# From the fourth step of a chunked scan on, each step's output products and the next step's Gram products form one set on the tensor engine

## The chip, the core and the metric

The kernel runs on one core of a Trainium2 chip. Its time is the device time of one execution in microseconds (us), here the median of three runs. The engines of the core work side by side and wait for one another through semaphores: PE (TensorE, matrix products; PEld is its weight loads), DVE (VectorE), ACT (ScalarE), POOL (GpSimd) and SP (SyncE, which issues the transfers). PSUM is the memory into which PE writes.

## The reference, cut to what matters

```python
# scan: 4 batches x 8 heads, 768 positions, head size 32, state size 16, in chunks
cum = np.cumsum(la, axis=-1)                       # la = log a of the chunk
L = np.exp(cum[:, :, :, None] - cum[:, :, None, :]) * causal
M = np.einsum('bhin,bhjn->bhij', Cc, Bc) * L       # the Gram products, then the decays
y[:, :, sl] = einsum(M, xc) + einsum(Cc, state) * exp(cum)
state = decay_full * state + sum_j(Bc * xc * decay_from_j)
# then, on the 3072 x 256 rows of y:
xn = x / rms * rms_g
x = (silu(xn @ w_gate) * (xn @ w_val)) @ w_out     # layer 1, d_ff 1536
h = x @ w_in
out = (s * relu(h)**2 + b) @ w_out2                # layer 2, d_ff 2048
```

## The kernel before

**The scan** goes in 16 steps of 48 positions. A step has two units (`NPAIR`; unit c belongs to step c // 2), each of which holds two batches with all 8 heads. A step consists of four functions, which `stream` lists in this order:

- `scan`: DVE's scan instruction makes the decays of the step in `a_sb`.
- `gram`: PE multiplies B by C (tiles `raw_bc`; `first_bc` in steps 0 and 1) into the columns 0 to 255 of both PSUM banks of the unit's tile `y`; then DVE multiplies these by the decays into `m`, four instructions for the two units (two 384 wide, two 128 wide).
- `outs`: PE multiplies `m` by the x tile `xh`, which also holds the state in 16 of its rows, into columns 256 to 511 of the first bank of `y`. ACT copies the new state into the next step's `xh` (`keep_state`), and DVE, POOL and ACT scale the rows to `xn`.
- `turn`: PE transposes `xn` against `ident` into columns 256 to 511 of the second bank, and ACT and DVE take these out as `xth` and `xtl`, the high and the low part of layer 1's input.

**The layers.** Layer 1 goes over the tokens in 7 blocks (4, 4, 4, 5, 5, 5, 5 units), each in 12 parts (products into `h`, then into `o`). Block 0 runs in plain float32 with weights `w1f`, which DVE and ACT decode from 64-bit words while it runs; the later blocks run as three products of split numbers (`w1h`, `w1l`). Layer 2 follows with tiles `h` and `acc`. The scan's steps lie between the products of the blocks whose tokens do not depend on them; the last `turn` of a block has to be done before that block's first product.

**The order of the instructions** is not that of the program text. Every call is recorded by a `Plan`, with a price and with the calls that it depends on; for PSUM it counts dependences by whole banks. `Plan.issue` then runs a list schedule over engines and transfers and issues the calls of each engine in the order of that schedule. Where it sees PE idle in the first microseconds, it puts in small bfloat16 products without a use (line 354). All other instructions have the line of the one call that issues them (358). `bundled` gives the small products of a step one group name, so that the planner keeps them together: "g" for Gram products, "o" for output products, "t" for transposes. The first product of a group takes over the dependences of all its members, with 0.6 us to spare.

The products of a group use the array in small pieces, which the trace prints as rows*columns: 32*64 for Gram products (16*64 in steps 0 and 1), 64*64 for output products, 128*128 for everything of the layers and for the transposes.

The Gram products read `raw_bc`, one buffer for all steps (398): a step's twelve transfers into it can start only when the Gram products of the step before have read it. The tile `y` comes from a pool of two buffers. Each unit asks for a new tile in `gram`, and so waits for everything that the unit two before it did with its tile.

Of the kernel before, what the change touches and what calls it, by code (L numbers as in the profile page):

```python
# [8 lines left out]
F32 = mybir.dt.float32  # L9
# [10 lines left out]
P = 128  # L20
# [8 lines left out]
NPAIR = 2  # L29
NUNIT = CPB * NPAIR  # L30
# [7 lines left out]
BLOCK = [j for j, n in enumerate(BLOCKS) for _ in range(n)]  # L38
NB = [n * UT for n in BLOCKS]
LAG = 2  # L40
F1 = 12
F2 = 16
N2 = 512
# [317 lines left out]
def place(k, h):  # L361

    return h % 2 * 4 + h // 2 if k % CPB < FREE // NPAIR else h


def chunk(c, z):

    p = c % NPAIR
    return (2 * p + (z ^ p)) * CPB + c // NPAIR
# [3 lines left out]
def scan_glu_relu2(ctx: ExitStack, tc: tile.TileContext, bc, xr, aa, cst, w1, w2, gn, sv, bv, out):  # L373
# [3 lines left out]
    const = ctx.enter_context(tc.tile_pool(name="const", bufs=1))  # L377
    wts = ctx.enter_context(tc.tile_pool(name="wts", bufs=F1))
    wlo = ctx.enter_context(tc.tile_pool(name="wlo", bufs=F2))
# [9 lines left out]
    s_p = ctx.enter_context(tc.tile_pool(name="s", bufs=3))  # L389
    hl_p = ctx.enter_context(tc.tile_pool(name="hl", bufs=LAG + 1))  # L390
    res_p = ctx.enter_context(tc.tile_pool(name="res", bufs=1))
    ps_h = ctx.enter_context(tc.tile_pool(name="ps_h", bufs=2, space=PS))
    ps_o = ctx.enter_context(tc.tile_pool(name="ps_o", bufs=1, space=PS))
    ps_y = ctx.enter_context(tc.tile_pool(name="ps_y", bufs=2, space=PS))
# [15 lines left out]

    w1h = [wts.tile([P, 6, P], F32R, tag="w1h", name="w1h") for m in range(F1)]
    w1f, w1l, w2f, w2h = {}, {}, {}, {}
# [6 lines left out]
    a_t, x_t, m_t, y_t, xn_t = {}, {}, {}, {}, {}  # L419
# [26 lines left out]
    def group(p, par):  # L446
        at = (2 * p + par) * 32
        return slice(at, at + NST)
# [23 lines left out]
    def load_x(c):  # L472
        t = x_p.tile([P, DM], F32, tag="xh", name="xh")
        for z in range(2):
            queue = nc.scalar if c < NPAIR else nc.sync
            queue.dma_start(out=t[z * R + NST:(z + 1) * R], in_=xr[chunk(c, z)])
            if c < NPAIR:
                nc.gpsimd.memset(t[z * R:z * R + NST], 0.0)
        x_t[c] = t
# [16 lines left out]
    def bundled(name, units, products, together=False):  # L496
        if units[0] >= FREE:
            nc.bundle = f"{name}{units[0]}"
        nc.fresh = True
        if together:  # L500
            products(units)
        else:
            for c in units:
                products(c)
                nc.fresh = nc.fresh or units[0] < FREE
        nc.bundle = None

    def gram_of(c):
        return y_t[c][:, :, 0:4 * R].rearrange("p a (b r) -> p a b r", b=4)

    def gram_products(units):
        g = [gram_of(c) for c in units]
        if units[0] < FREE:
            for q in range(NH // 2):
                for z in range(2):
                    for p in range(NPAIR):
                        for par in range(2):
                            rows = group(p, par)
                            nc.tensor.matmul(
                                out=g[p][z * R:(z + 1) * R, par, q],  # L520
                                lhsT=first_bc[rows, z ^ p, q * R:(q + 1) * R],
                                rhs=first_bc[rows, z ^ p, (4 + q) * R:(5 + q) * R], start=True, stop=True,
                                tile_position=((2 * p + par) * 32, z * R),
                            )
            return
        for q in range(2):
            cols = slice(q * R, (q + 1) * R)
            for z in range(2):
                for p in range(NPAIR):
                    for half in range(2):  # L530
                        at = (2 * p + half) * 32
                        raw = raw_bc[at:at + 32, z ^ p]
                        nc.tensor.matmul(
                            out=g[p][z * R:(z + 1) * R, half, 2 * q:2 * q + 2], lhsT=raw[:, 0, cols],
                            rhs=raw[:, 1:3, cols], start=True, stop=True, tile_position=(at, z * R),
                        )

    def gram(units):
        if units[0]:
            load_bc(units)  # L540
        for c in units:
            y_t[c] = ps_y.tile([P, 2, 512], F32, tag="y", name="y")
        bundled("g", units, gram_products, True)
        for c in units:
            g = gram_of(c)
            t = a_t.pop(c)
            m = att2.tile([P, NH, R], F32, tag="m", name="m")
            mv, tv = (v.rearrange("p (a b) r -> p a b r", a=2) for v in (m, t))
            nc.vector.tensor_tensor(out=mv[:, :, :, NST:R], in0=g[:, :, :, NST:R], in1=tv[:, :, :, 0:CH], op=ALU.mult)
            nc.vector.tensor_tensor(  # L550
                out=mv[:, :, :, 0:NST], in0=g[:, :, :, 0:NST],
                in1=tv[:, :, :, CH:AW].to_broadcast([P, 2, 4, NST]), op=ALU.mult,
            )
            m_t[c] = m

    def rows_of(c):
        return y_t[c][:, 0, 4 * R:4 * R + DM]

    def out_products(units):
        for h in range(NH):  # L560
            for c in units:
                for z in range(2):
                    rows, t = slice(z * R, (z + 1) * R), z ^ c % NPAIR
                    nc.tensor.matmul(
                        out=rows_of(c)[t * R:(t + 1) * R, h * HD:(h + 1) * HD],
                        lhsT=m_t[c][rows, place(chunk(c, 0), h)], rhs=x_t[c][rows, h * HD:(h + 1) * HD],
                        start=True, stop=True,
                    )

    def keep_state(c):  # L570
        for z in range(2):
            t = z ^ c % NPAIR
            copy = nc.scalar.copy if c >= NPAIR else nc.vector.tensor_copy
            copy(out=x_t[c + NPAIR][z * R:z * R + NST], in_=rows_of(c)[t * R:t * R + NST])

    def outs(units):
        for c in units:
            if c < NPAIR:
                load_x(c)
        for c in units:  # L580
            if c + NPAIR < NUNIT:
                load_x(c + NPAIR)
        if units[0] < FREE:
            nc.fresh = True
            for c in units:
                out_products([c])
                nc.fresh = True
        else:
            bundled("o", units, out_products, True)
        ss = att2.tile([P, NPAIR], F32, tag="ss", name="ss")  # L590
        if units[0] == 0:
            nc.first_back = len(nc.ops) - 1
        for c in units:
            if c + NPAIR < NUNIT:
                keep_state(c)
            xn = xn_t[c] = att2.tile([P, DM], F32, tag="xn", name="xn")
            nc.scalar.activation(
                out=xn, in_=rows_of(c), func=AF.Square, scale=DM ** -0.5, accum_out=ss[:, c % NPAIR:c % NPAIR + 1]
            )
        if units[0] == 0:  # L600
            nc.squares = len(nc.ops) - 1
        rs = att2.tile([P, NPAIR], F32, tag="rs", name="rs")
        nc.now_free = units[0] < FREE
        nc.vector.tensor_scalar(out=ss, in0=ss, scalar1=1e-6, scalar2=None, op0=ALU.add)
        nc.gpsimd.tensor_tensor(out=rs, in0=ss, in1=mhalf.to_broadcast([P, NPAIR]), op=ALU.pow)
        if units[0] == 0:

            nc.vector.tensor_copy(out=held, in_=rs)
            nc.held = len(nc.ops) - 1
        for c in units:  # L610
            nc.scalar.activation(out=xn_t[c], in_=rows_of(c), func=AF.Copy, scale=rs[:, c % NPAIR:c % NPAIR + 1])
# [134 lines left out]
    def out1(j, m, hi, lo):  # L746
# [3 lines left out]
        for t in range(2):  # L750
            three(o[t], w1h[m][:, 4 + t, :], w1l[m][:, 4 + t, :], hi, lo, m == 0, m == F1 - 1)
            if m == F1 - 1:
                evac1(o, t, j)
# [29 lines left out]
    def hidden1_plain(j, m, half):  # L783
# [13 lines left out]
        def out():  # L797
            o = [t[:, :NB[j]] for t in o_t[j, 1]]
            last = m == F1 - 1
            for t in range(2):  # L800
# [158 lines left out]
    def drain(n):  # L959
        while len(pending) > n:  # L960
            pending.popleft()()
# [64 lines left out]
    behind = 3  # L1026
    for i in range(F1 + behind):
        if i < F1:
            decode1(i)
            hidden1_plain(0, i, 0)  # L1030
            drain(LAG)
        tokens_to(count[1] + (count[3] - count[1]) * (i + 1) // behind if i < behind else
                  count[3] + (count[7] - count[3]) * (i + 1 - behind) // F1)
        if i >= behind:
            hidden1_plain(0, i - behind, 1)
            drain(LAG)

# [6 lines left out]
    for i, (layer, j, m) in enumerate(plan):  # L1044
# [13 lines left out]
        if layer == 2:  # L1058
            if m == 0 and (g := j + 1) * N2 < 2 * NPAIR * SEQ:
                split_rows(g)  # L1060
            if m % 2 == 0:
                seven(j, m // 2)
                drain(LAG)
            continue
        hidden1(j, m)
        drain(LAG)
        for (i0, n0), (i1, n1) in zip(marks, marks[1:]):
# [76 lines left out]
```

## Time and profile before

| | |
|---|---|
| median of 3 runs (range) | 633.78 us (631.43 to 634.2) |
| the profiled execution: its own time | 633.83 us |
| the profiled execution: span from first to last instruction | 631.8 us |
| PE busy | 621.4 us, 98% of the span |
| DVE busy | 484.2 us, 77% |
| ACT busy | 446.2 us, 71% |
| sets of Gram products in 32*64 pieces | 14 (steps 2 to 15) |

The profiled execution's own time is 2.0 us longer than its span, and close to the median. A product's row in the trace lasts longer than the array needs for it, since products overlap in the pipeline: what a product costs is read from the start of one row to the start of the next.

### The profile page before, as it was taken

Reading aid. Unit: us, or ns where it says so; the run is one execution under the profiler, and the core shown is the slowest. Engines: PE = TensorE matmul, PEld = TensorE weight load, DVE = VectorE, ACT = ScalarE, POOL = GpSimd, SP = SyncE. Lnnn points to the kernel's source line nnn. Section 1 sums busy time; section 2 is a strip of 40 time slices with the busy share of each in tenths; the row PEclk is TensorE's granted clock in tenths of the full one; section 3 lists DMA queues with packets and bytes.
Section 4 is the critical chain, followed back from the end, with each engine's and each line's share of the span. In section 5 each row is a group of like instructions: output and inputs, shape, how many; then the busy total and the mean of one; then the engine's idle time right before and its main releaser. Section 6 shows DMA issues by size and latency. Waiting matters only on the chain.

```text
span 631.8 us, 12985 instructions
## 1 busy us (share of the span) xinstructions
PE 621.4 (98%) x4979; PEld 556.4 (88%) x4979; DVE 484.2 (77%) x980; ACT 446.2 (71%) x940; POOL 50.6 (8%) x88
## 2 busy tenths in 40 slices
PE   8999999999999999999999999999999999999996
PEld 7899999999988888888888889999999999999986
DVE  7999956677757666756775568798897897987975
ACT  3797535666646545655655479899898898988985
POOL 3000000000101111101232220000000000000000
PEclk9899999999999999999999999999999999999999
DMA  7769203343413432500100000001010010010101
GB/s 224 211 221 269 62 1 61 85 96 91 114 35 89 90 91 59 138 15 4 40 2 1 0 2 1 1 1 35 1 34 1 2 34 1 4 32 1 34 1 34
DMA packets 33694, 35.00 MB, mean 55 GB/s; under 512 B 14048, under 2 KB 30048, under 8 KB 33632
## 3 DMA queue, kind: packets, MB, share of 16 engines
q1 hardware_dynamic: 32688, 33.71, 20.6%
q8 instruction: 39, 0.64, 0.4%
q10 hardware_dynamic: 944, 0.46, 0.2%
q14 instruction: 23, 0.19, 0.1%
HBM read 30.90 MB, written 3.25 MB: 54 GB/s over the span
## 4 chain that ended last, share of the span: by engine, by line
PE 95%; DVE 2%; ACT 1%; issue 0%; DVEq 0%
PE h L358 54%; PE o L358 22%; PE acc L358 13%; PE y L358 5%; PE o L354 1%; DVE w1f L358 1%; DVE e L358 0%; ACT xn L358 0%; PE ab L358 0%; DVE res L358 0%; DVE a_sb L358 0%; DVE xh L358 0%; ACT e L358 0%; ACT xth L358 0%; ACT xh L358 0%
## 5 line engine op out<-in xcount | busy, mean ns | idle before, releaser
L358 ACT CAST hi<-s 128x256 fp32r<-128x256 f32 (+2 forms) x168 | 79.1, 474 | 69.8 <-DVE s L358 67.6
L358 ACT ACTIVATE s<-h 128x512 f32<-128x512 f32 (+2 forms) x168 | 96.1, 572 | 35.4 <-PE h L358 32.3
L358 PE MATMUL h<-x1h,w2h 128*128 128x512 f32 x384 | 119.2, 392 | 0.0
L358 DVE TENSOR_TENSOR lo<-s,hi 128x256 fp32r<-128x256 f32 (+2 forms) x168 | 85.7, 511 | 30.0 <-ACT hi L358 27.2
L358 PE MATMUL h<-xtl,w1h 128*128 128x480 f32 (+1 forms) x288 | 106.7, 371 | 0.0
L358 PE MATMUL h<-xth,w1l 128*128 128x480 f32 (+1 forms) x288 | 106.6, 370 | 0.0
L358 PE MATMUL h<-xth,w1h 128*128 128x480 f32 (+1 forms) x288 | 106.1, 369 | 0.1
L358 PE MATMUL acc<-hi,w2c 128*128 128x256 f32 x448 | 82.0, 281 | 0.0
L358 PEld LDWEIGHTS h<-x1h,w2h 128*128 128x128 f32 x384 | 69.2, 188 | 12.2
L358 DVE TENSOR_TENSOR s<-h,s 128x480 f32<-128x480 f32 (+1 forms) x72 | 44.6, 619 | 43.7 <-PE h L358 43.5
L358 PE MATMUL h<-x1l,w2h 128*128 128x512 f32 x192 | 75.0, 391 | 0.0
L358 PEld LDWEIGHTS acc<-hi,w2c 128*128 128x128 f32 x448 | 71.0, 189 | 2.2
L358 DVE TENSOR_TENSOR added<-s 128x256 f32<-128x256 f32 x144 | 56.4, 419 | 13.5 <-ACT s L358 12.5
L358 PE MATMUL acc<-lo,w2c 128*128 128x256 f32 x224 | 63.2, 282 | 0.0
L358 ACT ACTIVATE s<-s 128x512 f32<-128x512 f32 x96 | 60.2, 633 | 1.9
L358 PEld LDWEIGHTS h<-xth,w1h 128*128 128x128 f32 x288 | 54.1, 188 | 6.6 <-DVE s L358 0.5
L358 PEld LDWEIGHTS h<-xtl,w1h 128*128 128x128 f32 x288 | 54.1, 188 | 6.3 <-issue 1.0
L358 PEld LDWEIGHTS h<-xth,w1l 128*128 128x128 f32 x288 | 54.1, 188 | 6.4 <-issue 0.5
L358 PE MATMUL o<-lo,w1h 128*128 128x480 f32 (+1 forms) x144 | 53.0, 368 | 0.0
L358 PE MATMUL o<-hi,w1l 128*128 128x480 f32 (+1 forms) x144 | 52.9, 368 | 0.0
L358 PE MATMUL o<-hi,w1h 128*128 128x480 f32 (+1 forms) x144 | 52.9, 367 | 0.0
L358 DVE TENSOR_TENSOR lo<-added,hi 128x768 fp32r<-128x768 f32 x48 | 45.9, 956 | 0.6 <-ACT hi L358 0.5
(98 smaller groups left out, 1093.2 us busy)
## 6 DMA issues: line engine op xcount, KB each, us to landing
raw<-in_w SPq DMA_DIRECT2D x12, 768.0 KB, 4.9
raw<-in_w SPq DMA_DIRECT2D x16, 512.0 KB, 3.5
a_sb<-a_scr SPq DMA_DIRECT2D x28, 196.0 KB, 3.8
xh<-in_xr SPq DMA_DIRECT2D x60, 48.0 KB, 1.9
raw_bc<-in_bc SPq DMA_DIRECT2D x56, 32.0 KB, 2.2
raw_bc<-in_bc SPq DMA_DIRECT2D x112, 16.0 KB, 2.9
out_t<-res SPq DMA_DIRECT2D x13, 96.0 KB, 1.8
out_t<-res SPq DMA_DIRECT2D x5, 144.0 KB, 2.1
```

Source lines behind the costliest of these rows:

```text
L354: self.nc.tensor.matmul(out=idle, lhsT=ones, rhs=ones, start=True, stop=True)
L358: getattr(engine, op["fn"])(*op["args"], **op["kw"])
```

## The change

`JOIN` is the first unit of step 4. Up to step 3, nothing but the tile changes. For steps 4 to 15 the Gram products of a step are no longer issued in its own `gram`; they stand in the `outs` of the step before, ahead of that step's output products and in the same group. With them the loads of `raw_bc` are recorded there. The two tiles `y` are taken once and stay for all steps, so that only accesses to the same bank order the steps.

```diff
+JOIN = 4 * NPAIR
...
-    def gram(units):
+    y_p = [ps_y.tile([P, 2, 512], F32, tag="y", name="y") for _ in range(NPAIR)]
+
+    def begin_gram(units):
         if units[0]:
             load_bc(units)
         for c in units:
-            y_t[c] = ps_y.tile([P, 2, 512], F32, tag="y", name="y")
-        bundled("g", units, gram_products, True)
+            y_t[c] = y_p[c % NPAIR]
+
+    def gram(units):
+        if units[0] < JOIN:
+            begin_gram(units)
+            bundled("g", units, gram_products, True)
...
         else:
-            bundled("o", units, out_products, True)
+            ahead = range(units[0] + NPAIR, units[0] + 2 * NPAIR)
+            if JOIN <= ahead[0] < NUNIT:
+                begin_gram(ahead)
+
+                def products(units):
+                    gram_products(ahead)
+                    out_products(units)
+                bundled("o", units, products, True)
+            else:
+                bundled("o", units, out_products, True)
```

The planner then makes another order on every engine. Three places of it follow.

**Place 1, steps 10 and 11.** On PE before: the Gram products of step 10 (`y<-raw_bc`), eleven products of layer 1, and the output products of step 10 (`y<-xh,m`).

```order
L358 MATMUL y<-raw_bc 64x128 x16
L358 MATMUL h<-xtl,w1h 128x480
L358 MATMUL h<-xth,w1h 128x480 x2
L358 MATMUL h<-xth,w1l 128x480
L358 MATMUL h<-xtl,w1h 128x480
L358 MATMUL o_509<-hi,w1h 128x480
L358 MATMUL o_509<-hi,w1l 128x480
L358 MATMUL o_509<-lo,w1h 128x480
L358 MATMUL o_510<-hi,w1h 128x480
L358 MATMUL o_510<-hi,w1l 128x480
L358 MATMUL o_510<-lo,w1h 128x480
L358 MATMUL y<-xh,m 64x32 x32
```

On PE after the change, where step 10's output products stand: the Gram products of step 11 come directly ahead of them. (The planner counts a float32 product once, and the trace twice: x16 here is x32 there.)

```order
L359 MATMUL o_494<-lo,w1h 128x480
L359 MATMUL h<-xth,w1h 128x480
L359 MATMUL y<-raw_bc 64x128 x16
L359 MATMUL y<-xh,m 64x32 x32
L359 MATMUL h<-xth,w1l 128x480
L359 MATMUL h<-xtl,w1h 128x480
```

On DVE before, the four products `m` of step 10 stand well behind the four `xtl` of the turn before them:

```order
L358 SCALAR_TENSOR_TENSOR xtl<-y,sb,xth 128x2x48 x4
L358 TENSOR_SCALAR e<-raw_563 128x512
L358 TENSOR_TENSOR lo<-s,hi 128x480
L358 TENSOR_SCALAR raw_563<-raw_563 128x512
L358 SCALAR_TENSOR_TENSOR w2f<-raw_563 128x512
L358 TENSOR_TENSOR e<-e,sg 128x512
L358 TENSOR_TENSOR m<-y,a_sb 128x8x48 x2
L358 TENSOR_TENSOR m<-y,a_sb 128x8x16 x2
L358 TENSOR_TENSOR s<-h,s 128x480
```

On DVE after the change they stand around them:

```order
L359 TENSOR_TENSOR lo<-s,hi 128x480
L359 TENSOR_SCALAR raw_543<-raw_543 128x512
L359 TENSOR_TENSOR m<-y,a_sb 128x8x48 x2
L359 SCALAR_TENSOR_TENSOR xtl<-y,sb,xth 128x2x48 x4
L359 TENSOR_TENSOR m<-y,a_sb 128x8x16 x2
L359 TENSOR_TENSOR s<-h,s 128x480
```

So one set of products on PE has become a neighbour of another, and DVE's block at a turn has grown by the four `m`.

**Place 2, step 1, at 18 to 25 us of the trace.** On DVE before, from the second part's decode (`w1f`) to the first `m` of step 1:

```order
L358 TENSOR_SCALAR e<-raw_139 128x768
L358 TENSOR_TENSOR e<-e,sg 128x768
L358 SCALAR_TENSOR_TENSOR w1f<-raw_138 128x768
L358 TENSOR_TENSOR w1f<-w1f,e 128x768
L358 TENSOR_TENSOR h_157<-h,h_157 128x192
L358 TENSOR_TENSOR m<-y,a_sb 128x8x48
L358 TENSOR_SCALAR raw_139<-raw_139 128x768
L358 TENSOR_TENSOR e<-e,sg 128x768
```

On DVE after the change:

```order
L359 SCALAR_TENSOR_TENSOR w1f<-raw_140 128x768
L359 TENSOR_TENSOR e<-e,sg 128x768
L359 TENSOR_SCALAR e<-raw_141 128x768
L359 TENSOR_TENSOR h_157<-h,h_157 128x192
L359 TENSOR_TENSOR m<-y,a_sb 128x8x48
L359 TENSOR_SCALAR raw_141<-raw_141 128x768
L359 TENSOR_TENSOR w1f<-w1f,e 128x768
L359 TENSOR_TENSOR e<-e,sg 128x768
```

The instructions are the same; the second half of the decode, `w1f<-w1f,e`, has moved behind the first `m`. On PE the twelve products without a use that stood behind step 1's Gram products are gone.

**Place 3, the last turn of block 0's time (step 3), at 76 to 79 us.** On PE before, from the transposes to the first products of block 1 (`w1h`, `xth`):

```order
L358 MATMUL y<-ident,xn 128x128 x4
L358 MATMUL o_133<-h_269,w1f 128x192
L358 MATMUL o_134<-h_269,w1f 128x192
L358 MATMUL o_133<-h_277,w1f 128x192
L358 MATMUL o_134<-h_277,w1f 128x192
L358 MATMUL h<-xth,w1h 128x384
```

On PE after the change:

```order
L359 MATMUL o_135<-h_271,w1f 128x192
L359 MATMUL y<-ident,xn 128x128 x4
L359 MATMUL o_136<-h_271,w1f 128x192
L359 MATMUL o_135<-h_273,w1f 128x192
L359 MATMUL o_136<-h_273,w1f 128x192
L359 MATMUL h<-xth,w1h 128x384
```

One of the four output products that stood between the transposes and block 1 now stands ahead of the transposes.

## Rows read from the trace of the kernel before

**Rows 1.** What PE waited for, from 34 us to the end (total, times, longest); the largest.

```profile
PE h L358 <- ACT xth L358: 0.5, 1, 0.5
```

**Rows 2.** PE in order of time, step 10: start, us, instruction.

```profile
205.22 0.38 PE L358 MATMUL h<-xth,w1l 128*128 128x480 f32 x1
205.53 0.69 PE L358 MATMUL y<-raw_bc 32*64 32x128 f32 x32
206.15 0.49 PE L358 MATMUL h<-xtl,w1h 128*128 128x480 f32 x1
206.48 0.59 PE L358 MATMUL h<-xth,w1h 128*128 128x480 f32 x2
...
208.43 0.38 PE L358 MATMUL o<-lo,w1h 128*128 128x480 f32 x1
208.74 1.14 PE L358 MATMUL y<-xh,m 64*64 64x32 f32 x64
209.81 0.48 PE L358 MATMUL h<-xth,w1l 128*128 128x480 f32 x1
210.13 0.38 PE L358 MATMUL h<-xtl,w1h 128*128 128x480 f32 x1
```

**Rows 3.** PE: the last output product of steps 0 and 10, and what follows.

```profile
10.55 0.22 PE L358 MATMUL y<-xh,m 64*64 64x32 f32 x1
10.70 0.39 PE L358 MATMUL ab<-a_cl,ident 128*64 128x196 f32 x2
...
209.66 0.22 PE L358 MATMUL y<-xh,m 64*64 64x32 f32 x1
```

**Rows 4.** Front, step 1: PE, then DVE.

```profile
18.41 1.06 PE L358 MATMUL y<-first_bc 16*64 16x64 f32 x64
24.65 1.12 PE L358 MATMUL y<-xh,m 64*64 64x32 f32 x32 [1.30 <-DVE m L358]
27.55 2.29 PE L358 MATMUL h<-xth,w1f 128*128 128x192 f32 x6
29.63 1.15 PE L358 MATMUL o<-h,w1f 128*128 128x192 f32 x4
...
19.10 0.96 DVE L358 TENSOR_TENSOR w1f<-w1f,e 128x768 f32<-128x768 f32 x1
20.25 0.55 DVE L358 TENSOR_TENSOR m<-y,a_sb 128x384 f32<-128x384 f32 x1
```

**Rows 5.** Stretches: us, busy us of PE, PEld, DVE, ACT, POOL, granted clock, DMA share, GB/s.

```profile
26.90:30.30 3.40, 3.40 (x25) 3.34 (x22) 2.39 (x6) 1.67 (x6) 1.33 (x1) 0.50 0.83 139
50.00:60.00 10.00, 10.00 (x119) 9.73 (x119) 10.00 (x22) 7.74 (x18) 1.27 (x1) 1.00 0.95 273
```

**Rows 6.** PE from step 3's turn to block 1's first products.

```profile
76.87 1.47 PE L358 MATMUL o<-h,w1f 128*128 128x192 f32 x8
78.04 0.47 PE L358 MATMUL h<-xth,w1h 128*128 128x384 f32 x1
...
78.82 0.44 PE L358 MATMUL h<-xth,w1h 128*128 128x384 f32 x1
```

**Rows 7.** The page's transfers: KB each, median us from issue to landing.

```profile
raw_bc<-in_bc SPq DMA_DIRECT2D x112, 16.0 KB, 2.9
```

**Rows 8.** SP in order of time, step 10's loads: start, us until the last is issued.

```profile
194.84 5.14 SPq L358 DMA_DIRECT2D raw_bc<-in_bc  x9
```

**Rows 9.** The turn ahead of step 10 and step 10's `m`: PE, ACT, DVE.

```profile
201.95 0.60 PE L358 MATMUL y<-ident,xn 128*128 128x128 f32 x4
202.37 1.04 ACT L358 ACTIVATE xth<-y,sb 128x96 fp32r<-128x96 f32 x4 [0.96 <-PE y L358]
202.97 1.01 DVE L358 SCALAR_TENSOR_TENSOR xtl<-y,sb,xth 128x96 fp32r<-128x96 f32 x4
206.32 1.42 DVE L358 TENSOR_TENSOR m<-y,a_sb 128x384 f32<-128x384 f32 x4
```

## The prediction

> **What bounds the kernel now.** I read the table first: PE is busy for 98% of the span, DVE for 77%. That alone does not make PE the bound, so next come its waits. From 34 us to the end it waited twice; the longer wait was 0.5 us [rows 1]. So from there on the time is what PE's instruction stream costs, and only three things can change it: the cost of the stream itself, new waits, and the granted clock.
>
> The cost shows in the order of time around step 10. Only the starts of rows are used. Between 206.48 and 208.43 us nine products of 480 columns start (the order at place 1 lists them), so one costs 1.95 / 9 = 0.217 us [rows 2]. Around a set of small products the step from one start to the next is longer. The product ahead of the Gram set takes 0.31 (0.09 too much), the set 0.62, and the first product behind it 0.33 (0.11 too much): 0.82 us for one visit. The output set likewise: 0.31 (0.09), 1.07, 0.32 (0.10), together 1.26 us. A step pays 2.08 us for two visits, and 0.20 of this is the way out of the first and the way into the second.
>
> Ahead of 34 us it is otherwise. PE waits 1.30 us for DVE's `m` at 24.65 [rows 4], and from 26.90 to 30.30 it is busy throughout at a granted clock of 0.50, so 1.2 GHz in place of 2.4 [rows 5].
>
> **The merged sets.** Twelve Gram sets (steps 4 to 15) move next to the output products of the step before. One visit then costs 0.09 + 0.62 + 1.07 + 0.10 = 1.88 us, provided that the switch from Gram to output products costs what leaving a set costs. That switch is in no row, since the two sets never touch. The nearest rows are step 0's last output product, which steps to a product of another small shape (128*64) in 10.70 - 10.55 = 0.15 us, and step 10's, which steps to a full 128*128 product in 209.81 - 209.66 = 0.15 us [rows 3]. A change between two small shapes costs as much as one to the full array, and 32*64 to 64*64 is a change of shape too. So I let the switch stand inside the 0.62, and take 0.20 us for each merge: 12 x 0.20 = **-2.4 us**. The other bound: with no pause at the switch the step would be that inside the set, 1.07 / 64 = 0.017 us; 0.13 more each, 12 x 0.33 = -4.0 us.
>
> The Trainium skill ("TensorEngine Tiling (Array Packing)", Key Properties) says that a change of tiling mode, not merely of tile, drains the engine. By that the joined set keeps one drain in its middle and the gain is the smaller sum, -2.4 and not -4.0; the two 0.15 us steps agree.
>
> **The tiles and the transfers.** `y` had two buffers for two units before, so keeping them moves nothing in memory, and costs nothing as long as the same accesses are done in time. The twelve loads of `raw_bc` need the read of the last Gram set behind them. Nine of them took SP 5.14 us [rows 8], 0.57 each, so twelve take 6.9, and the last lands some 2.9 later [rows 7]: with about 0.9 us from the set's start to the first issue, 10.7 us. By the order after the change the closest two merged sets (with the output products of steps 12 and 13) stand 40 products of 480 columns apart: 40 x 0.217 + 1.88 + about 0.45 for the transposes = 11.0 us. It fits by 0.3 us. Two other pairs have 42 and 44 products, so 0.4 and 0.9 us more. Behind these loads on SP stand four `xh`, for a set a step later, and two `a_sb`. I take zero; a landing 1 us late at these places would cost 0.7 + 0.3 = 1.0 us.
>
> **The front.** At place 2 `w1f<-w1f,e`, 0.96 us at 19.10, moves behind the first `m`, which began at 20.25 [rows 4]. But `m` cannot start before the Gram set of 18.41 has ended at 19.47, so DVE may idle a little where it did not, and its last `m` there, for which PE waits at 24.65, comes later: I take **+0.25 us**, bounds 0 and +0.9 (the whole instruction's worth). The twelve products without a use that are gone filled time in which PE waited anyway. Whether the half-clock stretch behind stays is open: at half speed 3.4 us do the work of 1.7, so it is worth at most 1.7 us either way. The same long wait precedes it in both orders, so I leave it as it is. Further on DVE is full (10.00 of 10.00 us between 50 and 60 [rows 5]), and the Gram set of step 2 and others move by some products, but no DVE instruction is added, and PE did not wait there before; zero.
>
> **Block 1's start.** Between the last transposes of block 0 and block 1's first product stood eight rows of `o<-h,w1f` (place 3 lists them as four). They take 78.04 - 76.87 = 1.17 us, 0.146 each [rows 6]. After, six stand there. The first two products of block 1 took 78.82 - 78.04 = 0.78 us, where two of 384 columns cost 2 x 0.217 x 0.8 = 0.35, so PE already waited 0.43 us for `xth`. `xth` comes no sooner with two rows less ahead: that wait grows by 2 x 0.146, with the switch **+0.33 us**; bound 0, if ACT is done earlier.
>
> **The sum.** -2.4 + 0.25 + 0.33 = -1.8 us. The profiled execution's own time is 633.83, the median 633.78, so either gives **632.0 us**. 0.5% of this kernel is 3.2 us, about what a measurement can tell from no change: under 630.6 would be faster, over 636.9 slower. My forecast is no change that can be told.
>
> **Rivals.**
> *No pause at the switch.* Only the 0.15 us steps between other shapes speak against it. -4.0 + 0.58 gives 630.4.
> *The clock at the front.* If the 3.4 us at half clock do not come, 632.0 - 1.7 = 630.3. For it: DVE's order and PE's fill products both change just ahead. Against: PE still waits there. If a second such stretch comes, as fewer products run before it, 633.7.
> *The merged set is late (the other side).* A merged set must wait for the step's `m`, and its Gram products also until `xtl` has been read out of the second bank. Before, the four `m` (1.42 us) came well after the four `xtl` (1.01), with other work of DVE between; now they are one block of 2.43 us [rows 9]. ACT began on the turn 202.37 - 201.95 = 0.42 us after its start, DVE 1.02 after. So the block ends between 1.02 + 1.01 + 0.3 (the two small `m`) = 2.3 and 0.42 + 2.43 = 2.9 us after the transposes. By the order nine of the twelve merged sets stand only 12 to 21 products behind their transposes, that is 0.4 + 12 x 0.217 = 3.0 us at the least, and 3.6 at 15. One instruction of DVE that runs over (`lo`, `s`: 0.65 us) uses this up, and every product of the layers behind the set waits too. From 0.2 us of waiting per merge the gain is gone; 0.3 at nine sets costs 2.7 and gives 634.7; 0.6 gives 637.4, slower. For it: DVE's block is closer than any before. Against: DVE is free for a quarter of the span, and PE waited nowhere for `m` after 34 us. The loads above add up to 1.0 at three sets, which alone decides nothing.
> *It does nothing.* If the way in and out is paid all the same inside the joined set, only the front's +0.58 and other shifts remain: 634.
>
> **Chances.** The forecast 0.50 (own range 630.8 to 633.4); no pause 0.12; no half-clock stretch 0.10; a second one 0.08; late sets 0.15, of which 0.07 beyond 636.9; nothing 0.05. Faster: 0.12 + 0.10 and a little of the forecast's edge, 0.24. Slower: 0.07 and a little for waits that I do not see, 0.09. Same: 0.67. The range has to reach the no-pause and no-stretch cases below and the small late sets above: 629.8 to 635.4. It leaves out both lower cases at once and the large waits.
>
> **What would show it.** Twelve rows of `y<-raw_bc` directly followed by `y<-xh,m`, with 0.31 before, about 1.7 for both, 0.32 behind. Right on the switch if the last Gram product steps to the first output product in 0.15 to 0.2 us, wrong if in under 0.05. Right on the waits if PE waits in no more than 1 us in all behind 34 us, wrong if `y<-raw_bc` or `y<-xh,m` carry waits for `m`, `xtl` or a transfer. At the front: the wait for `m` some 0.25 longer, the clock 0.50 for about 3.4 us. At block 1: some 0.75 us in place of 0.43 ahead of its second product. A clock below 1.00 elsewhere, or waits at the merged sets of over 0.2 us each, would make the forecast wrong.

## The result, and the profile after

The changed kernel takes 636.46 us (median of 10 runs, 635.41 to 638.59), the kernel before 633.54 us beside it (10 runs, 631.23 to 634.68): a ratio of 1.0058, 95% interval 1.0044 to 1.0073. It is slower by 0.6%. I had forecast 632.0 us and a range up to 635.4. The profiled execution took 635.41 us with a span of 633.6; against the one of before (633.83 and 631.8) that is 1.6 us more by its own time and 1.8 by the span.

PE's waits from 34 us on, the counterpart of [rows 1] (what waited, for what, total, times, longest):

```profile
PE h L359 <- DVE s L359: 0.7, 1, 0.7
PE y L359 <- DVE xtl L359: 0.6, 1, 0.6
PE h L359 <- ACT xth L359: 0.5, 1, 0.5
PE h L359 <- ACT h L359: 0.2, 1, 0.2
PE h L359 <- DVE h L359: 0.2, 1, 0.2
```

They add up to 2.2 us, where before there were 0.7 (0.5 and 0.2), and the prediction asked for no more than 1. This list shows only gaps in which PE had nothing in flight; most of the loss stands in none of its lines, as will be seen.

**The joined set costs what was forecast.** PE in order of time, where step 10's output products follow step 11's Gram products (start, us, instruction), for [rows 2]:

```profile
208.57 0.38 PE L359 MATMUL h<-xth,w1h 128*128 128x480 f32 x1
208.88 0.69 PE L359 MATMUL y<-raw_bc 32*64 32x128 f32 x32
209.51 1.14 PE L359 MATMUL y<-xh,m 64*64 64x32 f32 x64
210.57 0.49 PE L359 MATMUL h<-xth,w1l 128*128 128x480 f32 x1
210.90 0.38 PE L359 MATMUL h<-xtl,w1h 128*128 128x480 f32 x1
```

The steps are 0.31 in, 0.63, 1.06, and 0.33 out, against 0.217 for a product: 0.09 + 0.63 + 1.06 + 0.11 = 1.89 us for 2.08 before. The Gram products' 0.63 is as long as when a full-size product followed (0.62): the way out of the small pieces is paid at the switch too. The last Gram product steps to the first output product in 0.20 us, as forecast:

```profile
209.31 0.27 PE L359 MATMUL y<-raw_bc 32*64 32x128 f32 x1
209.51 0.26 PE L359 MATMUL y<-xh,m 64*64 64x32 f32 x4
```

What the prediction cites from the Trainium skill ("TensorEngine Tiling (Array Packing)", Key Properties), that a change of tiling mode drains the engine, agrees with these 0.20 us.

**The turn.** ACT, then DVE, then PE around the turn at 107.5 us and the joined set behind it (for [rows 9]; the number in brackets is how long the engine idled ahead of the row, and for whom):

```profile
107.94 0.34 ACT L359 ACTIVATE xth<-y,sb 128x96 fp32r<-128x96 f32 x1 [0.55 <-PE y L359]
108.91 0.57 ACT L359 ACTIVATE xth<-y,sb 128x96 fp32r<-128x96 f32 x2 [0.62 <-DVE m L359]
110.11 0.34 ACT L359 ACTIVATE xth<-y,sb 128x96 fp32r<-128x96 f32 x1 [0.63 <-DVE m L359]
...
108.31 0.56 DVE L359 TENSOR_TENSOR m<-y,a_sb 128x384 f32<-128x384 f32 x1 [1.82 <-ACT xth L359]
109.51 0.56 DVE L359 TENSOR_TENSOR m<-y,a_sb 128x384 f32<-128x384 f32 x1 [0.64 <-ACT xth L359]
109.99 1.03 DVE L359 SCALAR_TENSOR_TENSOR xtl<-y,sb,xth 128x96 fp32r<-128x96 f32 x4
110.94 0.48 DVE L359 TENSOR_TENSOR m<-y,a_sb 128x128 f32<-128x128 f32 x2
...
107.52 0.60 PE L359 MATMUL y<-ident,xn 128*128 128x128 f32 x4
111.43 0.99 PE L359 MATMUL y<-raw_bc 32*64 32x128 f32 x32
```

Before, the four `xth` ran in one piece of 1.04 us [rows 9]. Now ACT and DVE take turns: `xth`, `m`, `xth` twice, `m`, `xth`, one behind the other, although neither `m` nor `xth` needs what the other makes. Both read the second bank of the same tile `y`. The waits are in the issued program: of the 64 `m` in the trace, 17 carry a wait for ACT's semaphore, before none; of the 64 `xth`, 23 carry one for DVE's, before 8. So the last `m` ends at 111.42, 3.9 us after the transposes began, and the joined set begins at 111.43 and is stretched to 0.99 - 0.69 = 0.30 us more than the one above. The waits of ACT for `m` in the whole scan, 34 to 330 us (total, times, longest):

```profile
ACT xth L359 <- DVE m L359: 7.1, 14, 0.6
```

And of DVE, for the same stretch:

```profile
DVE a_sb L359 <- DMA a_sb<-a_scr: 10.2, 9, 2.1
DVE m L359 <- ACT xth L359: 7.6, 14, 1.8
```

The two waits for one another are in neither list of before; the wait for the decays was there, with 6.8 us in 6.

When the last `m` of a step ends is what decides. In the changed kernel four of the twelve joined sets are stretched, by 0.26 to 0.41 us. They are the four (at 111.4, 159.0, 253.9 and 265.1 us) whose last `m` ends less than 0.2 us ahead of the set's first product, or after it. At the other eight it has ended 0.4 us before or earlier, and each of these costs 1.88 or 1.89 us.

**Two places where it ends on PE.** At 214 us DVE's scan waits for its load; the `xtl` and `s` behind it are late, and PE's next `h` waits (order of time on DVE, then PE):

```profile
214.11 0.97 DVE L359 TENSOR_TENSOR_SCAN a_sb<-a_sb,delta 128x392 f32<-128x392 f32 x1 [2.08 <-DMA a_sb<-a_scr]
219.88 0.65 DVE L359 TENSOR_TENSOR s<-h,s 128x480 f32<-128x480 f32 x1
...
220.58 0.49 PE L359 MATMUL h<-xth,w1h 128*128 128x480 f32 x1 [0.70 <-DVE s L359]
```

And the last step's output products, which now stand 11 products behind their turn (23 before), find `xtl` unfinished (PE in order of time):

```profile
315.71 1.57 PE L359 MATMUL y<-xh,m 64*64 64x32 f32 x64 [0.62 <-DVE xtl L359]
```

**The front and block 1.** For [rows 4], PE at step 1's first output products:

```profile
24.58 1.12 PE L359 MATMUL y<-xh,m 64*64 64x32 f32 x32 [1.71 <-DVE m L359]
```

For [rows 5], the stretch at half clock (us, busy of PE, PEld, DVE, ACT, POOL, granted clock, DMA share, GB/s):

```profile
26.90:30.30 3.40, 3.40 (x23) 3.34 (x22) 2.31 (x6) 1.65 (x5) 1.33 (x1) 0.52 1.01 296
```

For [rows 6], PE from block 0's last output products into block 1:

```profile
79.30 1.14 PE L359 MATMUL o<-h,w1f 128*128 128x192 f32 x6
80.14 0.47 PE L359 MATMUL h<-xth,w1h 128*128 128x384 f32 x1
80.45 0.33 PE L359 MATMUL h<-xth,w1l 128*128 128x384 f32 x1
80.61 0.34 PE L359 MATMUL h<-xth,w1h 128*128 128x384 f32 x1
```

Step 1's output products start 0.07 us earlier than before, not 0.25 later (PE's wait for `m` is 0.41 longer, 1.71 for 1.30, since PE comes to it earlier); the clock does the same; and block 1's first two products take 80.61 - 80.14 = 0.47 us for 0.78 before.

**Where PE's time went.** The layers' products are the same in both kernels and come in the same order, so they can be counted. For each row of PE I take the step to the next row's start, less what a product of its kind takes (0.163 us for 192 columns, 0.175 for 384, 0.2175 for 480), 0.82, 1.26 or 1.88 us for a Gram set, an output set or a joined set, and 0.44 or 0.22 for four or two transposes. What is left is lost time. Its growth over the kernel before, between numbered products (their times in the changed kernel's trace below them):

```
products              0-48   48-480  480-840  840-1260  1260-1500 | 48-1500  joined  time 48-1500
up to (us)            34     119     196      301       358
changed kernel        0.0    1.0     0.5      2.0       1.1       | 4.6      12      +2.2
```

The last column is the time by which product 1500 comes later, counted from product 48. It is 4.6 lost less 12 x 0.20 by the way the loss is worked out, so the sum itself proves nothing; that a joined set costs 1.88 is read from the sets' own rows. Behind product 1500 PE's rows run alike; what follows PE's last product is 0.3 us shorter, so the spans differ by 1.8 us.

### The profile page after: what moved, and what is told of

It reads as the page before. It is cut to its first block, busy times and chain, and to the rows that moved or that the text cites. A ratio compares the mean times of both kernels' runs of the same rounds, so it can differ in the third digit from the quotient of the medians.

```text
span 633.6 us, 12944 instructions
## 1 busy us (share of the span) xinstructions
PE 621.5 (98%) x4967; PEld 556.8 (88%) x4967; DVE 484.2 (76%) x980; ACT 447.5 (71%) x940; POOL 54.0 (9%) x88
## 4 chain that ended last, share of the span: by engine, by line
PE 85%; DVE 7%; ACT 3%; DMA 2%; issue 1%; POOL 0%; SPq 0%; DVEq 0%; POOLq 0%
PE h L359 48%; PE o L359 19%; PE acc L359 13%; PE y L359 4%; DMA a_sb<-a_scr 2%; DVE w1f L359 1%; DVE e L359 1%; DVE a_sb L359 1%; ACT xth L359 1%; DVE m L359 1%; PE o L355 1%; DVE xtl L359 1%; ACT xn L359 1%; DVE raw L359 1%; DVE s L359 0%
```

## The experiments

All medians are of 10 to 12 runs beside the kernel before on the same chip (6 for e7), ratios to it with 95% intervals.

| run | median | ratio (95%) |
|---|---|---|
| e1 tiles kept, no joins | 633.38 | 0.9984 (0.9970 to 0.9997) |
| e2 m after xth | 635.89 | 1.0037 (1.0025 to 1.0049) |
| e3, e5 early m | 633.34, 633.31 | 0.9988 (0.9972 to 1.0004), 0.9999 (0.9985 to 1.0013) |
| e4, e14 joins from step 9 | 636.06, 636.01 | 1.0029 (1.0013 to 1.0044), 1.0035 (1.0017 to 1.0053) |
| e13 the same, m after xth | 634.01 | 0.9998 (0.9980 to 1.0016) |
| e6, e15 the same, early m | 632.0, 632.84 | 0.9979 (0.9963 to 0.9995), 0.9987 (0.9971 to 1.0004) |
| e7 decays loaded first | 648.54 | 1.0233 (1.0205 to 1.0261) |
| e8 early m, two decay buffers | 631.58 | 0.9976 (0.9961 to 0.9991) |
| e9 joins of steps 4 and 5 alone | 634.69 | 1.0019 (1.0002 to 1.0035) |
| e10 early m from step 6 | 630.5 | 0.9964 (0.9944 to 0.9984) |
| e11 early m from step 8 | 632.45 | 0.9982 (0.9965 to 1.0000) |
| e12 as e10, two decay buffers | 630.86 | 0.9952 (0.9936 to 0.9968) |

PE's lost time over the kernel before, read from each one's trace as above:

```
products              0-48   48-480  480-840  840-1260  1260-1500 | 48-1500  joined  time 48-1500
e1                   -2.1    0.0     0.0      0.0       0.0       | 0.0       0      0.0
e2                    0.3    0.9     2.0      0.4       1.1       | 4.4      12      +2.0
e5                    0.8    1.5    -0.3     -0.1       0.2       | 1.3      12      -1.1
e9                   -2.2    1.6     0.2      0.0       0.0       | 1.8       2      +1.4
e14                   1.0    0.0    -0.5      2.3       1.5       | 3.3       7      +1.9
e13                  -2.2    0.0    -0.5      0.8       1.1       | 1.4       7      0.0
e15                  -2.2    0.0     0.7     -0.1       0.2       | 0.9       7      -0.5
e10                  -2.0    0.9     0.1     -0.1       0.2       | 1.0      10      -1.0
```

The last column is again the loss less 0.20 us for each joined set, by the way it is worked out. That the gain is there is shown by the sets: in e5 and in e7 each of the twelve costs 1.88 to 1.90 us. The traces of e4 and e6, the kernels of e14 and e15, give losses of 4.0 and 1.4 behind product 48, so two traces of one kernel differ by 0.5 to 0.7 us. The first column is the front, of which below.

**e1: the tiles alone.**

```diff
-JOIN = 4 * NPAIR
+JOIN = NUNIT
```

> Only the two tiles y are kept; no set is joined. Theory (readers in turn: ScalarE's xth and VectorE's m read the same PSUM tile at a turn and are made to wait for one another, which the planner does not count; the joined sets and the s products pay for it): as before, 633.5 us, within 0.8, and no wait of ScalarE for m. Rival 1 (crowding: the m merely lengthen VectorE's block at a turn): the same. Rival 2 (the front is what costs): the same. Rival 3 (keeping the tiles costs by itself): near 636.

633.38 us. Counted from product 48, its trace stands within 0.01 us of before at products 480, 840, 1260 and 1500, and never more than 0.34 us away: keeping the tiles costs nothing. Rival 3 falls.

**e2: m after xth.** The planner gets one more dependence for the `m` of a joined step (first line, in `gram`), on the last activation that writes `xth` of that unit's turn one step earlier (second line, in `turn`).

```diff
+            nc.after = turned.get(c - NPAIR) if units[0] >= JOIN else None
...
+                turned[c] = len(nc.ops) - 1
```

> The change, and the planner is told that a joined step's m come after the four xth of the turn, so that the two engines no longer take turns. Readers in turn: the waits of ScalarE for m at the turns vanish, more than half of the 3.7 us that PE loses behind 100 us goes, about 634 us. Crowding: the m stay in the block of the turn, so no gain, 636 to 637. Front: no gain, 636 to 637.

635.89 us: above the 634 of the theory, hardly below the changed kernel. ACT's waits for `m` in the scan did go, from 7.1 us in 14 to

```profile
ACT xth L359 <- DVE m L359: 1.4, 3, 0.5
```

and between products 840 and 1260 so did four fifths of the loss (0.4 for 2.0 us). But the planner's new order put two scans where their loads came late, with `lo` and `s` queued behind them on DVE, and PE lost 1.9 us between 158 and 171 us, 1.5 of it behind the first. The joined set there waits 0.3 us for a load of `xh` besides. DVE in order of time:

```profile
153.39 1.84 DVE L359 TENSOR_TENSOR_SCAN a_sb<-a_sb,delta 128x392 f32<-128x392 f32 x2 [1.72 <-DMA a_sb<-a_scr]
166.33 1.84 DVE L359 TENSOR_TENSOR_SCAN a_sb<-a_sb,delta 128x392 f32<-128x392 f32 x2 [1.33 <-DMA a_sb<-a_scr]
```

As a time it does not decide; e13 repeats it where this does not happen.

**e3 and e5: early m.** A joined step's scan and `m` are recorded ahead of the turn of the step before. Until then the planner held them to come after that turn's transposes, since it counts dependences by whole banks and the transposes write a bank that the `m` read.

```diff
-            s += [(6 * c + t, units, f) for t, f in zip((2, 4, 8), (scan, gram, outs))]
+            s += [(6 * c + t, units, f) for t, f in zip((0, 1, 8) if c >= JOIN else (2, 4, 8), (scan, gram, outs))]
```

> The change, with a joined step's scan and m recorded ahead of the turn of the step before, so that its m no longer count as depending on that turn's transposes and can run before them. Readers in turn: no alternation is left, the 2.4 us of the joined sets show: 632 to 633.5 us. Crowding: the same, since the m leave the block. Front: 635.5 or more, since block 0 stays as changed.

633.34 us, 3.1 below the changed kernel. e5 is the same kernel once more, for its trace:

> The kernel of the early m once more, for a profile at the full clock. If the m in the turn's block were what cost: no wait of ScalarE for m and none of VectorE's m for xth; PE's lost time between 100 and 320 us falls from about 4.2 us over the kernel before to under 1.5, and 0.8 us is still lost in block 0. If the late loads of a_sb matter as much: waits for them stay near 10 us on VectorE and PE still loses 2 us or more there.

633.31 us. ACT's `xth` waits nowhere for `m`, and PE's waits behind 34 us are

```profile
PE h L359 <- ACT xth L359: 0.7, 1, 0.7
PE h L359 <- DVE ss L359: 0.3, 1, 0.3
PE o L359 <- DVE h L359: 0.2, 1, 0.2
```

Behind product 480 it loses nothing (-0.3, -0.1, 0.2), where the changed kernel lost 3.6 us; up to there, in block 0 and at the start of block 1, it loses 1.5. So its joins give 2.4 and cost 1.3. The waits for `a_sb` fell as well, to 2.5 us in 4, against what the second case of the expectation said. The edit moves the scan with the `m`, so this kernel alone does not tell the one from the other.

**e4: joins from step 9 on.** `JOIN = 9 * NPAIR`.

> Sets joined from step 9 on only: 7 joined sets, front and blocks 0 to 3 as before. Readers in turn, crowding: the joins give back 1.4 us and the waits behind them cost about 2.9, as in the changed kernel's trace from 190 us on: 635 us. Front: the waits of blocks 0 and 1 are gone, 632 us.

636.06 us, a point for the turn's block and against the front: with seven joins, and with block 0 and the start of block 1 (up to product 363) issued as before, it is nearly as slow as the changed kernel.

**e6: the same with early m.**

> Early m and joined sets from step 9 on only (7 sets): block 0 as before. If block 0's new order costs the early version its 0.8 us and the joins are then free: 633.8 less 1.4, so 632.4 us, a little below the version joined from step 4. If the joins cost as much as they bring wherever they stand: 633.8.

632.0 us as the first case has it, 4 us below e4, which differs in the place of the scan and the `m` alone.

**e7: the loads of the decays first.**

```diff
+        if units[0] >= JOIN:
+            load_a(units)
+            sent, nc.sent = nc.sent, nc.ops[-1]
+            load_bc(units)
```

> The change with the loads of a_sb for a joined step queued on SyncE ahead of that step's raw_bc, which are kept in one order. The planner then spaces the steps more widely and puts all four m ahead of the xtl. If the a_sb loads behind sixteen others cost a part: no wait of VectorE for a_sb over 1 us, and 633 us or less. If the m beside the turn are all that costs: the same as the early m, about 633.3. If neither: 636.

648.54 us, none of the three. Holding the loads in one order made the planner lay out block 0 anew, and PE had lost some 11 us by product 300 there. It says nothing on the loads. It does say what the waits cost by themselves: `m` and `xth` still waited for one another (8.0 us in 21 on DVE, 8.8 in 16 on ACT), but every joined set stands 10 us or more behind its last `m`, and none is stretched.

**e8: two buffers for the decays, with early m.** `SLOTS = 2 * NPAIR`, and the scan in two halves.

> Early m, and two buffers for each unit's decays (the scan instruction is split in two to make room, 28 more instructions of VectorE), so that a_sb of the next step is loaded a step ahead. If waiting for a_sb holds up what is behind the scan on VectorE: its waits for the load vanish, and it is 0.5 to 1.5 us below the early m, about 632. If not: the same or, by the split scans, up to 0.5 us more.

631.58 us, 1.7 below e3 and e5. But DVE still waits 6.0 us for `a_sb`, more than in e5, and PE loses 2.7 us behind product 48, also more: the reason given for it is not what happened. Its trace has no half-clock stretch at the front; product 48 starts 2.0 us earlier than before, where in e5 it starts 0.8 later, and the profiled execution (631.69 us) is close to the median. So what this version gains over e5 in the traces stands at the front.

**e9: the joins of steps 4 and 5 alone.** `END = 6 * NPAIR` in place of `NUNIT`.

> Only the sets of steps 4 and 5 are joined (the two that stand in block 0 and at the start of block 1); from step 6 on the order of before. Turn's block (m beside xth and xtl): little of the loss stands here; the changed kernel's trace lost 0.4 to 0.7 us gross up to 105 us against 0.4 gained, so 634 us. Front: if block 0's new order and its clock carry the loss, 636.

634.69 us, between the two. Its trace loses 1.8 us and gains 0.4, but not where the joins stand: up to product 430, at 105 us, it loses 0.4, as the changed kernel does. Another 1.2 us stand at step 5's own output products. They have no Gram set ahead of them here, stand 15 products behind their turn and find `xtl` unfinished:

```profile
109.47 1.57 PE L360 MATMUL y<-xh,m 64*64 64x32 f32 x64 [0.66 <-DVE xtl L360]
```

The row is the same as that of step 15 in the changed kernel, at 315.71: where the joins end, the last output products come too early.

**e10 and e11: early m, joins from step 6 or 8 on.** `JOIN = 6 * NPAIR`, `JOIN = 8 * NPAIR`.

> Early m, joined sets from step 6 on (10 sets, gain 2.0 us), block 0 as before. Turn's block: the early version lost 1.8 us up to 105 us and nothing behind it, so without the joins in block 0 most of the 2.0 shows: 631.8 us. Front of no account: 633.3, as the early version.

> Early m, joined sets from step 8 on (8 sets, gain 1.6 us). Turn's block: between the versions from step 9 (632.0) and from step 6, 632 us. Front of no account: 633.3.

630.5 and 632.45 us. e10 beats both kernels. By its trace the joins are worth 1.0 of the 3.4 us between the medians. 7 of its 12 executions lie between 629.6 and 630.9 us, the profiled one, which has no half-clock stretch, among them; of the 32 of before beside it 7 lie between 630.9 and 631.9. These low groups differ by 1.3 us; the rest of the 3.4 comes mostly of how many executions lie in them. e11's time is e6's within their spread.

**e12: early m, two decay buffers, joins from step 6.**

> Early m, two buffers for the decays (scan split in two), joined sets from step 6 on. If both the joins in block 0 and the late a_sb cost a part, they add up: 631 us, the fastest so far. If they are the same cost told twice: 631.6 to 632.

630.86 us, with the lowest ratio of all, but it cannot be told from e10: that the two costs add up is not shown.

**e13 to e15: the cause, on one chip.** Joins from step 9, issued as before up to product 363, and only the place of the `m` (in e15 of the scan too) differs: as in the change (e14), after `xth` (e13, the edit of e2), early together with the scan (e15). e13 and e14 issue the same up to product 722, at 167 us.

> Joined sets from step 9 on, and each unit's m after its two xth. Alternation: ScalarE's waits for m vanish and most of PE's loss behind 170 us with them, 1.5 to 2.5 us below the same joins without it, near 634. The m in the turn's block, whatever their order: no gain, 636.

> Joined sets from step 9 on, otherwise as the change, for the comparison on one chip: 636 us as measured there before.

> Early m, joined sets from step 9 on, for the comparison on one chip: 632.0 us as measured there before. By the alternation alone it is little below the version with m after xth; by the block it is some 4 us below it.

636.01, 634.01 and 632.84 us, in the order e14, e13, e15. Telling the planner of the one dependence gives back 2.0 of the 3.2 us that the place of the `m` costs; the other 1.2 are not clear of the noise (the intervals of e13 and e15 overlap). The same joined set in both, with the transposes (PE) and the last `m` (DVE) ahead of it, in e14:

```profile
205.01 0.60 PE L359 MATMUL y<-ident,xn 128*128 128x128 f32 x4
208.45 0.48 DVE L359 TENSOR_TENSOR m<-y,a_sb 128x128 f32<-128x128 f32 x2
208.89 1.03 PE L359 MATMUL y<-raw_bc 32*64 32x128 f32 x32
```

ACT's waits for `m` and DVE's for the decays between 170 and 320 us in e14:

```profile
ACT xth L359 <- DVE m L359: 5.6, 10, 0.7
DVE a_sb L359 <- DMA a_sb<-a_scr: 4.1, 3, 2.2
```

The same in e13:

```profile
201.68 0.60 PE L359 MATMUL y<-ident,xn 128*128 128x128 f32 x4
205.02 0.48 DVE L359 TENSOR_TENSOR m<-y,a_sb 128x128 f32<-128x128 f32 x2
205.91 0.69 PE L359 MATMUL y<-raw_bc 32*64 32x128 f32 x32
```

```profile
ACT xth L359 <- DVE m L359: 0.4, 1, 0.4
DVE a_sb L359 <- DMA a_sb<-a_scr: 5.8, 5, 2.3
```

In e14 the set starts 3.88 us after the transposes at 205.01 and is stretched by 0.34; in e13 it starts 4.23 us after those at 201.68 and is not. The last `m` ends about as late in both (3.9 and 3.8 us after the transposes). So the engines are not much faster without the alternation; what changes is that the planner, which now counts the `m` behind the `xth`, puts the set where they are done and other products ahead of it. Three joined sets are stretched in e14, by 0.27 to 0.44 us, and one in e13, by 0.15. The waits for the decays are longer in e13 than in e14, so they are not what it gives back.

## Why the prediction was wrong

**The gain: right.** The joined set costs 1.89 us as worked out, with the pause at the switch, so 0.20 us less than two visits; in e5 all twelve cost 1.88 or 1.89. The rival without a pause is out: it asked for under 0.05 us at the switch, which takes 0.20.

**The waits: the step that failed.** "It costs nothing as long as the same accesses are done in time" is true of the tiles (e1) and was the wrong question. The late set, to which I gave 0.15, is what happened. I had put the end of DVE's block at 2.3 to 2.9 us after the transposes, by adding up durations as if `m` could run beside `xth`, and from this the sum took nothing for waits. At the four stretched sets the block ended 3.7 to 3.9 us after them, since `m` and `xth` read one tile and wait for one another, 14 times each way. In e13, where all `m` come behind the `xth`, it ended at 3.8: it is that they do not run side by side which counts, in whatever order. The Trainium skill ("PSUM — Partial Sum Buffer", PSUM bank collisions raise a hardware error) states the rule that I did not weigh: two engines may not be in one PSUM bank at once, two readers included, and software adds a dependence between them. The trace agrees, with ACT 0.62 and 0.63 us idle for `m` at that turn. The planner leaves it out too: it counts two readers of a bank as independent, so it puts the sets earlier than their `m` can be done. This is shown by e13 beside e14 (2.0 us), and the early `m` agree (3.1 us below the change, nothing lost behind product 480). The loss is not the same at each set, as my price for this case had it: four joined sets are stretched by 0.26 to 0.41 us, one `h` comes 0.86 us late, and step 15's output products lose 1.1 us, of which e5 loses 0.2. That last place, the output products at the end of the joins, I had not looked at.

**The decays' loads: not seen.** I had worked out the loads of `raw_bc`, which arrived in time at every joined set. It is `a_sb`, behind them on SP, that DVE waits for, 10.2 us for 6.8 before; in e2 and at 214 us of the changed kernel this reaches PE. It is a part of the loss, whose size no run separates, since e7 and e8 did not do what they were meant to; the 2.0 us between e14 and e13 are not of it.

**The front: sign wrong, size small.** +0.25 at step 1 was -0.07, and +0.33 at block 1's start was -0.31. The zero that I took for the rest of block 0 was wrong too: DVE is full there [rows 5], and the products behind three `o` come 0.33, 0.34 and 0.16 us late (at 52.6, 62.2 and 66.5 us). With what only the kernel before loses there, 0.4 us are left up to product 430, as much as the joins of steps 4 and 5 give.

**The rest.** The two profiled executions differ by 1.6 us, the medians by 2.9. Six of the changed kernel's ten executions list a mean granted clock of 0.993, the profiled one 0.995. A longer stretch at half clock at the front of the others could give a part of the difference, but no trace of them shows it; two list 0.997 and took 636.45 and 636.89 us; and the mean takes in the end of the kernel as well (e4's is 0.997 with 1.00 between 24 and 34 us and 0.79 from 626 us on). This stays open.

## What to carry to other kernels

Before moving work next to other work, list what reads the same PSUM tile on other engines: two readers on two engines were kept in turn here, whatever they need of one another, and the four `xth` that took 1.04 us took 2.5, which no sum of durations has. When a hand-written planner decides the order, look at the waits that the issued program carries, not at the order alone, and compare them with the dependences that the planner counts. And a merge that saves 0.2 us on the bounding engine is worth making only where what feeds it is done in time: with the `m` moved out of the turn and block 0 left alone, ten of the twelve joins brought 1.0 us on PE, and the kernel was faster than both.

## What was not expected of the hardware

The stretch at half clock at the front comes and goes with the same instructions. e14 and e15 issue the same instructions there; between 26.9 and 30.3 us the window of e14 is (columns as above)

```profile
26.90:30.30 3.40, 3.40 (x24) 3.34 (x21) 2.09 (x6) 1.63 (x5) 1.33 (x1) 0.50 1.05 224
```

and that of e15

```profile
26.90:30.30 3.40, 3.40 (x23) 3.21 (x22) 3.23 (x7) 3.34 (x9) 1.33 (x1) 1.00 1.04 214
```

It is 1.2 GHz in e14 and 2.4 in e15, with PE busy throughout in both; ahead of it PE waits 1.24 us for `m` in both. A part of the difference stands earlier still: the first sixteen `ab` products, of e14 and then of e15, take

```profile
4.53 2.14 PE L359 MATMUL ab<-a_cl,ident 128*64 128x196 f32 x16 [0.40 <-issue]
4.53 1.55 PE L359 MATMUL ab<-a_cl,ident 128*64 128x196 f32 x16 [0.59 <-issue]
```

and 2.44 in the profile of before. Why is not shown. Product 48 starts at 35.3 us in e14, at 34.4 in the profile of before and at 32.2 in e15. e1, which issues what the kernel before issues, starts it at 32.2 as well and ends 2.1 us earlier than the profile of before; e4 and e14, the same kernel, differ by 0.5 us between products 48 and 480. So in these traces most of what the kernel before spreads over, 631 to 635 us, arises in the first 35 us, and a difference of 0.3% between two medians can be no more than how often the front was slow.
